# Linear attention and gated MLP on one core: query blocks in seven products for eight, and instruction orders computed from one program text

## The chip, the cores and the metric

One core of a Trainium2 chip. The metric is the device time of one execution in microseconds, lower is better. The kernel before takes 208.9 us (median of three runs, 208.53 to 208.99).

A core has TensorE (PE, matmuls into PSUM), VectorE (DVE), ScalarE (ACT), GpSimd (POOL) and SyncE (SP, which here only issues DMAs). Each runs its own list of instructions in order; between engines there are semaphores. PSUM is used as eight banks of 512 float32 columns per partition.

## What is computed

One input `x` of 2048 tokens by 640 features, bf16. A layer norm without weights gives `xn`, which goes two ways: linear attention with 32 heads of 20 features, and an MLP of width 1728 whose output, through silu, gates the attention's.

```python
xn = _layernorm(x)
q, k, v = split(xn @ wqkv)                       # 32 heads of 20
phi = lambda t: where(t > 0, t + 1, exp(t)) + 1e-6
pq, pk = phi(q), phi(k)
kv, z = einsum("bhsd,bhse->bhde", pk, v), einsum("bhsd->bhd", pk)
o = einsum("bhqd,bhde->bhqe", pq, kv) / (einsum("bhqd,bhd->bhq", pq, z)[..., None] + 1e-6)
s = o @ wo
g = silu(relu(xn @ w1) @ w2)
out = x + s * g
```

## The kernel before

Tokens are cut into 16 tiles `t` of 128, or four chunks `j` of 512. The work, in the order of TensorE:

- **Head.** `x` and weights are loaded; `bn`, `aggr` (statistics) and `LN_norm` (normalisation, VectorE) make `xn`; `xnT_dma` (L545) turns each tile by a transposing DMA on SP. Key tiles (`K_mm`, L551, ten matmuls of 320 columns) are evacuated by ScalarE twice, exp and relu (`K_evac`), and `K_fin` on VectorE adds them to `pk`. Hidden blocks (`H_mm`, L655) are five matmuls of 512 columns and a relu.
- **Hidden and query blocks.** Ten pairs of hidden feature tiles are computed in *units* (`h_unit`, L1002), each a two by two block product in seven products for eight (Winograd's form). Sums of weight blocks (`h_S`) and of `xnT` blocks (`h_T`) are made beforehand by VectorE in float16. A unit has seven steps: s1, s5, s6, s2, s7, s3, s4. It holds four PSUM banks; s1, s5 and s7 are followed by a copy on ScalarE, s6 and s4 by an addition on VectorE that reads PSUM. Query blocks (`Q_mm`, L607; feature tile `f` of five, chunk `j` of four: 20 blocks of five matmuls) and key tiles 8 to 15 stand between the steps as fillers, so that TensorE has work while the other engines evacuate. `Q_mm` is followed by exp and relu on ScalarE and two operations on VectorE.
- **Denominator and gram matrix.** `z_sum`, `z_col`, `den`, `den_rec`: the reciprocal of the denominator goes to DRAM and is read back spread over partitions (`den_store`, `load_recip`, chunk by chunk), and `divide` multiplies the queries by it. `xn`'s gram product with `pk` takes two units (`seven`, gram) and a last feature tile directly (L1580); from it and `wv`, `kv_group` and `W_block` build the attention's output weight `wf`, whose rows are put in place by ten small DMAs.
- **Output.** Eight pairs of token tiles: `U_steps` (MLP's second matmul, in seven products, gates by silu) and `O_steps` (attention output, in seven products, for pairs 1 to 6; tiles 0, 1, 14 and 15 directly by `s_tile` and `s_last`), then `s_mult` and `s_store` on VectorE and the output's DMA.

All orders are written out by hand: the Python code calls `sc.op`, `sc.group` and `sc.dma` in one sequence, and each engine gets its instructions in that sequence. `Sched` works out the waits at each call. `K_mm` with `whole=True` adds one matmul of 192 columns (L562) that only fills the rest of a bank.

The order around the first query block, after key tile 7 in the head: x load of tiles 10 and 11, hidden blocks 4, 5, 10, 11, 12 of chunk 1 with normalisation 8, x loads 12 to 15 and two w1 loads between them, `H_half`, then query blocks (0,0) and (0,1).

Of the kernel before, what the change touches and what calls it, by code (L numbers as in the profile page):

```python
# [11 lines left out]
class _Res:  # L12
    __slots__ = ("w", "r", "nread")

    def __init__(self):
        self.w = None
        self.r = {}
        self.nread = 0


class Sched:

    def __init__(self, nc, n_dma_sems):
        self.nc = nc
        self.ops = {E: [] for E in ENGS}
        self.count = {E: 0 for E in CENGS}
        self.gseq = 0
        self.seq_at = {E: [] for E in CENGS}
        self.seq_at_dma = []
        self.vc = {E: {} for E in ENGS}  # L30
        self.vc_at = {E: [] for E in CENGS}
        self.vc_at_dma = []
        self.res = {}
        self.ndma = 0
        self.dma_sem_of = []
        self.dsem_count = [0] * n_dma_sems
        self.dsem_last_k = [None] * n_dma_sems
        self.n_dma_sems = n_dma_sems
        self.allow_unread = set()

# [18 lines left out]
    def _require(self, E, agents, waits):  # L59
        need_eng = {}  # L60
        need_dma = []
        for a in agents:
            if self._known(E, a):
                continue
            if a[0] == "D":
                if a not in need_dma:
                    need_dma.append(a)
            else:
                if need_eng.get(a[0], -1) < a[1]:
                    need_eng[a[0]] = a[1]  # L70
        items = [("E", Ep, idx, self.seq_at[Ep][idx]) for Ep, idx in need_eng.items()] + \
                [("D", a[1], None, self.seq_at_dma[a[1]]) for a in need_dma]
        items.sort(key=lambda x: -x[3])
        for kind, a1, a2, _sq in items:
            if kind == "E":
                Ep, idx = a1, a2
                if self._known(E, (Ep, idx)):
                    continue
                waits.append(("E", Ep, idx + 1))
                vc = self.vc[E]  # L80
                vc[Ep] = max(vc.get(Ep, 0), idx + 1)
                self._merge(E, self.vc_at[Ep][idx])
            else:
                k = a1
                if self._known(E, ("D", k)):
                    continue
                si, val = self.dma_sem_of[k]
                waits.append(("D", si, val))
                self.vc[E][("D", k)] = True
                self._merge(E, self.vc_at_dma[k])  # L90

    def _hazards(self, R, W):
        agents = []
        for key in R:
            st = self.res.get(key)
            if st is not None and st.w is not None:
                agents.append(st.w)
        for key in W:
            st = self.res.get(key)
            if st is not None:  # L100
                if st.w is not None:
                    agents.append(st.w)
                agents.extend(st.r.values())
        return agents

    def _update_res(self, agent, R, W):
        Rset = set(R)
        for key in R:
            st = self.res.get(key)
            if st is None:  # L110
                st = self.res[key] = _Res()
            rk = agent if agent[0] == "D" else agent[0]
            st.r[rk] = agent
            st.nread += 1
        for key in W:
            st = self.res.get(key)
            if st is None:
                st = self.res[key] = _Res()
            else:
                assert (st.w is None or st.nread > 0 or key in Rset or key in self.allow_unread  # L120
                        or (agent[0] == "PE" and st.w[0] == "PE")), (
                    "unread overwrite of %r by %r (prev writer %r)" % (key, agent, st.w))
            st.w = agent
            st.r = {}
            st.nread = 0

    def op(self, E, fn, R=(), W=(), extra=()):
        return self.group(E, [fn], R, W, extra)

    def group(self, E, fns, R=(), W=(), extra=()):  # L130
        assert E in CENGS
        waits = []
        agents = self._hazards(R, W) + list(extra)
        self._require(E, agents, waits)
        idx = self.count[E]
        self.count[E] += 1
        self.vc_at[E].append(dict(self.vc[E]))
        self.seq_at[E].append(self.gseq)
        self.gseq += 1
        self.ops[E].append(("op", waits, fns, idx))  # L140
        self._update_res((E, idx), R, W)
        return (E, idx)

    def dma(self, E, fn, sem_idx, R=(), W=(), extra=()):
        waits = []
        agents = self._hazards(R, W) + list(extra)
        prev = self.dsem_last_k[sem_idx]
        if prev is not None:
            agents.append(("D", prev))
# [14 lines left out]
    def wait_all_dma(self, E, sem_idxs):  # L164
        waits = []
        for si in sem_idxs:
            k = self.dsem_last_k[si]
            if k is None:
                continue
# [1527 lines left out]
```

## Time and profile before

| what | value |
|---|---|
| median of 3 runs | 208.9 us |
| span of the profiled execution, first to last instruction | 207.0 us |
| last matmul ends | 204.5 us |
| matmuls | 1400 |
| granted TensorE clock, mean | 1.000 |

The span is what the page and the trace describe; the runs' times hold some 1.9 us around it. In a row of instructions the first two numbers are start and duration in us, counted from the span's start; where several are merged, the duration runs from the first's start to the last's end. Matmuls overlap in the pipe (one of 512 columns lasts 379 ns by its row), so the distance between starts, not the duration, is what one costs.

### The profile page before, as it was taken

The page shows a single profiled execution, that of the slowest core. Times are in us where ns is not written, and L with a number is a line of the kernel's source. Part 1 is how long each engine was busy: PE and PEld are TensorE (multiplying, and loading weights), DVE is VectorE, ACT ScalarE, POOL GpSimd, SP SyncE. Part 2 cuts the span into 40 slices and gives each one's busy share as a digit, 9 for nine tenths or more (in the row PEclk, how much of TensorE's full clock was granted, in tenths as well). Part 3 has the DMA queues.
Part 4 walks back from the last instruction along what each step waited for, and adds up shares of the span by engine and source line. Part 5 has one row for each costly group of instructions (what it writes and reads, how often), then busy time and mean ns, then how long its engine had stood idle before and what let it go on. Part 6 is the DMA issues. An engine that isn't in the chain of part 4 may idle for free.

```text
span 207.0 us, 3745 instructions
## 1 busy us (share of the span) xinstructions
PE 203.6 (98%) x1400; PEld 126.3 (61%) x1400; DVE 169.7 (82%) x373; ACT 124.3 (60%) x251; POOL 18.0 (9%) x53
## 2 busy tenths in 40 slices
PE   8999999999999999999999999999999999999995
PEld 7755645545555444444456777777777777777773
DVE  4888997988969787686889669898888989897465
ACT  5598869888889987686563435462525354352531
POOL 3174032101330000000000000000000000000001
PEclk9999999999999999999999999999999999999999
DMA  6965999211037000302225999237931011010103
GB/s 194 331 190 117 255 203 275 42 32 29 6 63 198 25 3 0 127 0 57 74 63 114 251 357 384 90 108 234 371 129 63 3 63 46 21 63 0 63 5 127
DMA packets 32999, 24.74 MB, mean 119 GB/s; under 512 B 12757, under 2 KB 32981, under 8 KB 32981
## 3 DMA queue, kind: packets, MB, share of 16 engines
q1 hardware_dynamic: 31749, 23.13, 39.2%
q10 hardware_dynamic: 1232, 1.37, 1.9%
q8 instruction: 11, 0.18, 0.4%
q14 instruction: 7, 0.06, 0.1%
HBM read 15.81 MB, written 5.24 MB: 102 GB/s over the span
## 4 chain that ended last, share of the span: by engine, by line
PE 97%; DMA 1%; DVE 1%; issue 0%
PE psT L882 40%; PE psT L1036 19%; PE psT L556 11%; PE psT L609 11%; PE psT L658 6%; PE psT L1529 3%; PE psT L1580 2%; DMA reg<-in_A_x_dram 1%; PE psT L676 1%; PE psT L1320 1%; PE psT L530 1%; PE psT L1294 1%; PE psT L756 1%; PE psT L786 1%; PE psT L432 0%; DVE stats L469 0%
## 5 line engine op out<-in xcount | busy, mean ns | idle before, releaser
L882 PE MATMUL psT<-reg,regH 128*128 128x320 bf16 (+1 forms) x224 | 34.3, 299 | 0.0
L882 PE MATMUL psT<-reg 128*128 128x320 bf16 (+1 forms) x164 | 27.7, 299 | 0.0
L882 PEld LDWEIGHTS psT<-reg,regH 128*128 128x128 bf16 (+1 forms) x224 | 21.9, 98 | 8.6
L1354 ACT ACTIVATE wv_sb<-psT 128x320 bf16<-128x320 f32 x28 | 11.3, 436 | 25.2 <-PE psT L882 15.4
L609 PE MATMUL psT<-reg 128*128 128x512 bf16 x100 | 24.4, 379 | 0.0
L1036 PE MATMUL psT<-reg 128*128 128x512 bf16 x80 | 23.2, 379 | 0.0
L827 DVE TENSOR_TENSOR psT<-psT,reg 128x320 f32<-128x320 f32 x30 | 14.3, 493 | 9.3 <-PE psT L882 9.2
L889 ACT ACTIVATE psT<-psT 128x320 f32<-128x320 f32 x32 | 13.6, 426 | 11.2 <-PE psT L882 10.7
L882 PEld LDWEIGHTS psT<-reg 128*128 128x128 f16 (+1 forms) x164 | 16.0, 98 | 6.9 <-DVE regH L827 0.2
L889 ACT ACTIVATE reg<-psT 128x320 f32<-128x320 f32 (+1 forms) x24 | 10.4, 435 | 15.6 <-PE psT L882 13.6
L556 PE MATMUL psT<-reg 128*128 128x320 bf16 x120 | 17.9, 299 | 0.0
L1042 ACT ACTIVATE psT<-psT 128x512 f32<-128x512 f32 x20 | 11.9, 595 | 8.2 <-PE psT L1036 8.2
L569 ACT ACTIVATE regE<-psT 128x640 bf16<-128x640 f32 x24 | 15.6, 706 | 1.9 <-PE psT L556 1.2
L609 PEld LDWEIGHTS psT<-reg 128*128 128x128 bf16 x100 | 9.6, 98 | 11.6 <-issue 0.7
L1048 ACT ACTIVATE regH<-psT 128x512 bf16<-128x512 f32 (+1 forms) x24 | 14.5, 604 | 2.1 <-PE psT L1036 1.8
L556 PEld LDWEIGHTS psT<-reg 128*128 128x128 bf16 x120 | 11.5, 98 | 6.5 <-ACT regE L569 0.5
L469 DVE BATCH_NORM_STATS2 stats<-reg 128x6 f32<-128x320 bf16 x32 | 14.1, 475 | 1.3 <-DMA reg<-in_A_x_dram 1.3
L827 DVE TENSOR_TENSOR reg<-reg 128x1024 f16<-128x1024 bf16 (+6 forms) x17 | 13.5, 805 | 1.7 <-DMA reg<-in_B_w_dram 1.2
L882 PE MATMUL psT<-reg,pqT 128*128 128x320 bf16 (+1 forms) x72 | 14.7, 299 | 0.0
L1517 DVE TENSOR_TENSOR reg<-psT,wv_sb 128x640 bf16<-128x640 f32 (+2 forms) x16 | 11.8, 739 | 3.0 <-PE psT L882 1.8
L1036 PEld LDWEIGHTS psT<-reg 128*128 128x128 bf16 x80 | 7.7, 98 | 9.4 <-issue 0.4
L1522 POOL TENSOR_TENSOR reg<-reg 128x224 bf16<-128x224 bf16 x1 | 0.6, 607 | 144.0 <-DVE reg L1517 144.0
(143 smaller groups left out, 369.0 us busy)
## 6 DMA issues: line engine op xcount, KB each, us to landing
reg<-in_B_w_dram SPq DMA_DIRECT2D x12, 320.0 KB, 5.5
scr<-rden SPq DMA_DIRECT2D x4, 640.0 KB, 8.3
reg<-in_A_x_dram SPq DMA_DIRECT2D x4, 640.0 KB, 6.6
out_dram<-reg SPq DMA_DIRECT2D x15, 160.0 KB, 1.9
regE<-scr SPq DMA_DIRECT2D x3, 640.0 KB, 7.5
reg<-in_A_x_dram SPq DMA_DIRECT2D x4, 320.0 KB, 4.4
reg<-in_A_wo_dram SPq DMA_DIRECT2D x6, 160.0 KB, 3.3
reg<-in_A_x_dram SPq DMA_DIRECT2D x5, 160.0 KB, 5.5
```

The lines of the kernel that those rows point to most:

```text
L469: sc.op("DVE", lambda eng: eng.bn_stats(stats[:, t, a, :], xv[:, HN * a:HN * (a + 1)]), R=[("xin", xs(t))], W=[("stats", t, a)])
L556: fns.append(lambda eng, a=a, k=k, lhs=lhs: eng.matmul(ps[b + a][:, 0:HN], lhsT=lhs, rhs=wk[:, k, HN * a:HN * (a + 1)], start=(k == 0), st ...
L569: sc.op("ACT", lambda eng: eng.activation(out=o_.rearrange("p (a n) -> p a n", a=2), in_=ps2(b, HN), func=func, scale=scale), R=[("ps", b) ...
L609: sc.group("PE", [(lambda eng, k=k: eng.matmul(ps[b], lhsT=wq[:, k, P * f:P * (f + 1)], rhs=xnT[:, j, k, :], start=(k == 0), stop=(k == C ...
L658: sc.group("PE", [(lambda eng, k=k: eng.matmul(ps[b], lhsT=w1_col(k, P * f, P), rhs=src[:, k, :], start=(k == 0), stop=(k == C - 1))) for ...
L827: sc.op("DVE", lambda eng: eng.tensor_tensor(out=out, in0=in0, in1=in1, op=op), R=R, W=W, extra=extra)
L882: sc.group("PE", [(lambda eng, k=k, lhs=lhs, rhs=rhs: eng.matmul(ps[b][:, 0:HN], lhsT=lhs, rhs=rhs, start=(start and k == 0), stop=(k == n ...
L889: sc.op("ACT", lambda eng: eng.activation(out=dst, in_=ps[b][:, 0:HN], func=ACTF.Copy), R=[("ps", b)], W=[dkey], extra=extra)
L1036: sc.group("PE", [(lambda eng, k=k, lhs=lhs, rhs=rhs: eng.matmul(ps[b], lhsT=lhs, rhs=rhs, start=(start and k == 0), stop=(k == n - 1), sk ...
L1042: sc.op("ACT", lambda eng: eng.activation(out=dst, in_=ps[b], func=ACTF.Copy), R=[("ps", b)], W=[dkey], extra=extra)
L1048: sc.op("ACT", lambda eng: eng.activation(out=dst, in_=ps[b], func=ACTF.Relu), R=[("ps", b)], W=[("hT", j, f)])
L1517: sc.op("DVE", lambda eng: eng.tensor_tensor(out=tmpo[:, os_, lo:hi].rearrange(shp, a=na), in0=src, in1=g_of(t)[0][:, lo:hi].rearrange(shp ...
```

## The change

It has one new algorithmic part and moves nearly all of the order.

- **Query units.** `q_unit(f, jp)`, for f of 0 and 1 and both chunk pairs, computes the blocks (f, f+2) by (2jp, 2jp+1) in seven products: sixteen of 20 query blocks. `q_S` makes the sums of `wq` blocks; the sums of `xnT` are those of the hidden units, of which there are now two sets (`hTv[0]`, `hTv[1]`). The four blocks of feature tile 4 stay direct. (`k_unit` and `m_unit`, for keys and a mixed pair, are defined and not used in the text.)
- **One program text.** After the head, `PROGRAM` lists the steps by name. `play` reads it word by word. Banks are no longer fixed: `take` gives the free bank that was used longest ago, units get the half of PSUM that is free.
- **Computed order.** Calls only record. `Sched.place` then goes through all records with a duration for each kind (`cost`) and takes, for ScalarE, VectorE and GpSimd, the next one among the first 60 recorded by earliest start and latest allowed time. TensorE and SP keep the order of the text, and so does everything of the head. Orders are static in the built kernel.
- **Key tiles 8 to 15 in halves** (`K_half`, 320 columns, one bank each; four ScalarE instructions a tile for two), without the `whole` matmul.
- **DMAs.** On SP, `n8` (normalisation 8 and its transposing DMA) comes ahead of x loads 10 to 15, `n9` ahead of x load 12, and so on, by the text. `wo` is loaded after w2 instead of early. `wv` comes in two parts. Reciprocals: do0, do1, rc0, do2, rc1, do3, rc2, rc3, with W_block's copies and the reload of `x` between them.
- **End.** Tile 14 (`st14`) comes after the last step of the last unit.

```diff
+    def place(self):
...
+            for E in ENGS:
...
+                if E in ("PE", "SP") or w[0].n < self.head:
+                    c = w[0]
...
+                else:
+                    can = [(max(free[E], ready[o.n]), o.late, o.n) for o in w[:self.LOOK] if not nleft[o.n]]
...
+                    est, late, n = min(can)
+                    c = recs[n]
+                    for e2, l2, n2 in can:
+                        if l2 < c.late and (e2 <= est or (e2 < est + c.occ and l2 < est + c.occ)):
+                            c, est2 = recs[n2], e2
...
+    LOOK = 60
...
+    if name in ("tensor_copy", "tensor_scalar", "memset"):
+        return (0.065 + 0.00105 * n, 0.15 + 0.00105 * n) if wide else (0.08 + 0.00026 * n, 0.16 + 0.00026 * n)
...
+            o.occ = 1.3 if o.turn else 0.5
...
+            o.dur = 2.7 if o.turn else 1.95 + o.byt
...
+PROGRAM = """
+H15 n8 xa H111 T0 xc n9 xb rb n10 H14 SQ H112 Q04 a1.s5 a1.s1 H110 p0.s5 wa Ka8 n11 wb a1.s6 n12 a1.s2 n13
+p0.s1 n14 a1.s7 a1.s3 p0.s2 SH1 a1.s4 Kb8 p0.s6 n15 Ka9 Kb9 p0.s3 a0.s1 Ka10 Q14 p0.s7 a0.s5 a0.s6 Kb10 a0.s2
+p0.s4 a0.s7 T1 hh0 Kb12 a3.s1 a0.s3 a0.s4 a3.s5 a3.s6 Ka11 a3.s2 Kb11 a3.s7 a3.s3 b3.s1 b3.s5 a3.s4 b3.s6
...
+H212 b1.s5 b1.s2 GS0 b1.s6 a2.s5 a2.s1 b1.s7 b1.s3 a2.s6 b1.s4 SH2 a2.s2 b0.s5 b0.s1 a2.s3 a2.s7 b0.s6 b0.s2
...
+b2.s3 b4.s1 b4.s5 b2.s4 g0.s5 w2b g0.s1 b4.s2 b4.s6 mv6 g0.s6 b4.s3 b4.s7 hh1 g0.s2 b4.s4 g0.s7 dn w2d g0.s3
+w2c g0.s4 c0 GS1 sl wo uSa0 g1.s1 g1.s5 g1.s6 g1.s2 g1.s7 g1.s3 g1.s4 wv1 wv0 do0 do1 c1 uT1 u0.s1 kv1 uT3 rc0
+uSb0 dv0 do2 rc1 kv0 uT2 uT4 u0.s5 u0.s6 W2 W5 u0.s2 W1 do3 u0.s3 oS1 W3 u0.s7 uSa1 W0 W4 xre u1.s1 uSb1 rc2
+dv1 uSa2 oT u0.s4 u1.s5 u1.s6 u1.s2 u2.s1 u1.s3 u1.s7 u2.s5 u1.s4 st1 st0 o1.s5 uSa3 u2.s2 o1.s1 oS2 u2.s6 rc3
...
+o5.s3 uSb7 u6.s4 o5.s4 u7.s1 o6.s5 u7.s5 o6.s1 u7.s6 o6.s2 u7.s2 o6.s6 u7.s7 o6.s3 o6.s7 u7.s3 o6.s4 u7.s4
+st14
+"""
...
+    def q_S(i):
+        A11, A12, A21, A22 = wq[:, 0:2, 0:2 * P], wq[:, 2:4, 0:2 * P], wq[:, 0:2, 2 * P:4 * P], wq[:, 2:4, 2 * P:4 * P]
...
+            tt(qSv[1], A21, A22, ALU.add, [("wq",)], [k(1)])
...
-    def h_unit(i, jp=1):
+    def unit(jp, blk, wkeys_, ws, skeys, out, out22, tile=None):
...
             1: (z([blk(0, 0), blk(0, 1)], xb(j0, 0)), w),
             2: (z([blk(0, 2), blk(0, 3)], xb(j0, 2)) + last(0, j0), w),
+            3: (z(ws(4), xb(j1, 2)) + last(0, j1), w + sk(4)),
+            4: (z([blk(1, 2), blk(1, 3)], tv(4)) + last(1, j0), w + [("hTs", jp, 4)]),
+            5: (z(ws(1), tv(1)), sk(1) + [("hTs", jp, 1)]),
+            6: (z(ws(2), tv(2)), sk(2) + [("hTs", jp, 2)]),
+            7: (z(ws(3), tv(3)), sk(3) + [("hTs", jp, 3)]),
             8: (last(1, j1), w),
...
+    def q_unit(f, jp):
+        o = P * f
+
+        def out(half, j, b):
+            both, sum_ = Q_evac(j, f + 2 * half, b)
+            both()
+            pend.append(sum_)
+
+        def out22(j, b, s5, skey):
+            tt(ps[b], ps[b], s5, ALU.add, [("ps", b), skey], [("ps", b)])
+            out(1, j, b)
...
+    def take(narrow=False):
+        can = [b for b in range(8) if held[b] is None and (b % 2 or not narrow)]
+        assert can, "no free bank"
+        b = min(can, key=lambda b: (last_use[b], b))
+        last_use[b] = step_no[0]
+        return b
...
+    def K_half(t, a):
+        b = take(True)
+        K_mm(t, [b, b], halves=(a, ))
+        for func, slot, key in ((ACTF.Exp, 0, "ek_e"), (ACTF.Relu, 1, "ek_r")):
+            sc.op("ACT", lambda eng, func=func, slot=slot: eng.activation(
+                out=ek[:, eks(t), slot, HN * a:HN * (a + 1)], in_=ps[b][:, 0:HN], func=func),
+                R=[("ps", b)], W=[(key, eks(t), 1)] if a else [(key, eks(t))])
...
+    def norm(t):
+        if t > 8:
+            S(t)
+        N(t)
...
+        "xa": lambda: x_load(10, 2),
+        "xb": lambda: x_load(12, 2),
+        "xc": lambda: x_load(14, 2),
...
+        "wv0": lambda: w_load(wv_sb[:, 0:2, :], A_wqkv[0:2 * P, 2 * D:3 * D], ("wv", 0), extra=hz([("s5h", 0)]), E="ACT"),
```

In the text `a` and `b` are hidden units on chunks 0 and 1, and 2 and 3; `p` and `q` query units likewise; `g` gram units; `u` and `o` output units; `Hjf` and `Qjf` direct blocks; `Ka8`, `Kb8` the halves of key tile 8; `rb` the row scales' four small matmuls (L943); `hh` the half feature tile; `T` and `SH`, `SQ` sums of `xnT` and of weights; `wa`, `wb` loads of w1; `dv`, `do`, `rc` divide, store and load of reciprocals.

## The prediction

> **What bounds the kernel now.** I read the page's busy table, its slices and its chain first, since they tell which engine sets the end.
>
> ```profile
> PE 203.6 (98%) x1400; PEld 126.3 (61%) x1400; DVE 169.7 (82%) x373; ACT 124.3 (60%) x251; POOL 18.0 (9%) x53
> ...
> PEclk9999999999999999999999999999999999999999
> ...
> PE 97%; DMA 1%; DVE 1%; issue 0%
> ```
>
> TensorE is busy for the whole span at the full granted clock and is 97% of the chain. A busy matmul row can still hide waiting, so next came the timeline of TensorE, for the distance from start to start.
>
> ```profile
> 40.80 0.57 PE L556 MATMUL psT<-reg 128*128 128x320 bf16 x3
> 41.21 0.25 PE L562 MATMUL psT<-reg,const-bfloat16-1.0 128*128 128x192 bf16 x1
> 41.29 0.60 PE L1036 MATMUL psT<-regX,pqT 128*128 128x512 f16 x2
> 41.73 0.81 PE L1036 MATMUL psT<-reg 128*128 128x512 bf16 x3
> 42.37 1.24 PE L609 MATMUL psT<-reg 128*128 128x512 bf16 x5
> 43.45 0.59 PE L1036 MATMUL psT<-regX,reg 128*128 128x512 f16 x2
> ```
>
> Five 512-column matmuls of L609 take 43.45 - 42.37 = 1.08 us, so 0.2165 us each; ten of 320 columns go by at 0.136 us each in the same way. Nothing stands between the groups. From about 8 us to 204.5 I find no hole over 0.2 us. TensorE's work is the time, then: what is taken from it is gained whole, what is not cannot be gained, and every new wait of TensorE is lost whole.
>
> **What is removed.** A query unit computes four of the 20 blocks (feature tiles f and f+2, token chunks j0 and j1) with 18 matmuls of 512 columns (products of 2, 3, 3, 3, 2, 2, 2 and 1) where direct blocks take 4 x 5 = 20. Four units save 8 x 0.2165 = 1.73 us. The `whole` matmul of L562 goes; the next start is 41.29 - 41.21 = 0.08 us later, four times: 0.32 us. I count the other matmuls of the program text against the loops: key halves, hidden units, gram units, `u` and `o` units, the four direct output tiles are as many as before. Floor: -2.05 us.
>
> **The first query block.** TensorE follows the text word by word. After the last key tile of the head it has H15, H111, the four matmuls of `rb`, H14, H112, then Q04. The rows that price this:
>
> ```profile
> 23.45 2.32 PE L658 MATMUL psT<-reg 128*128 128x512 bf16 x10
> 25.61 0.39 PE L943 MATMUL psT<-ident,rsyH 128*128 128x128 bf16 x4
> 25.83 3.40 PE L658 MATMUL psT<-reg 128*128 128x512 bf16 x15
> ...
> 26.15 1.28 SPq L546 DMA_TRANSPOSE reg<-reg  x1
> ...
> DMA to landing us min/median/max: 2.7/2.7/2.7
> ```
>
> Q04 is reached at 23.45 + 4 x 1.083 + 0.22 = 28.0 (in the old order a fifth H block, 1.19 us of `H_half` and so 30.36). It reads `xnT` of tiles 0 to 3. The last of these four transposing DMAs is issued at 26.15 and lands 2.7 later, at 28.87, and everything ahead of it on SP (two loads, three transposes) belongs to the head, which stays in its order. So TensorE waits 0.9 us. Bounds: 0, if the four land a microsecond earlier, as they may with fewer loads in flight, and 1.2 (their slowest neighbour was issued over 2.04 instead of 1.28). I take 0.9. The transposes that are moved ahead of loads (`n8` before `xa`, `n9` before `xb`) come behind these four on SP and can't help them; they help Ka8, 4.5 us after Q04, whose tile is due in time: `n8` issues at 27.5 instead of 28.10 and before the loads that stretched its landing.
>
> *A rule beside it.* The Trainium skill (Advanced Engine Details and Errata, X-Bar Transpose (TRN2)) says that transposing DMAs are as fast as plain ones. By that rule the wait is not there and the sum ends 0.9 lower. The trace speaks against it: 1.28 us on SP for a transpose of 160 KB, 0.43 to 0.58 for plain loads.
>
> **VectorE and ScalarE after the head.** The units add, each, three copies (0.60 us, 0.49 from start to start), two 512-column PSUM additions (0.70, 0.61 apart); the sums of `q_S` are four of 0.42. ScalarE: 12 x 0.49 = 5.9, and eight key tiles in halves, 8 x (4 x 0.33 - 2 x 0.59) = 1.1, both from the distances of such instructions in the timeline. VectorE: 8 x 0.61 + 4 x 0.35 = 6.3. Stages before:
>
> ```profile
> 26.00:54.60 28.60, 28.60 (x165) 14.26 (x164) 24.97 (x64) 23.54 (x44) 5.55 (x12) 1.00 0.48 106
> 54.60:111.00 56.40, 56.40 (x352) 27.93 (x351) 45.19 (x97) 43.22 (x81) 2.50 (x10) 1.00 0.20 56
> 111.00:124.00 13.00, 13.00 (x96) 9.17 (x95) 9.69 (x16) 4.13 (x10) 0.00 (x0) 1.00 0.99 281
> ```
>
> The columns are TensorE, weight loads, VectorE, ScalarE, GpSimd, clock, DMA share. The tight place is the first row: the text puts `b3.s5`, which needs tiles 8 to 15 transposed and the first sum of `T1`, 25.7 us of TensorE's work after Q04, at 54.6, where the old kernel began such units at 72. VectorE must do by then: K_fin of tiles 6 to 9, 4 x 0.77 = 3.1; eight norms 2.9; seven statistics 7 x 1.04 = 7.3; `T0` 2.5 and 0.6 of `T1`; nine weight sums 3.2; a1, a0 and a3's first sum 3.6; p0 with four block sums 3.9; one of the two single blocks' and p0's six sums may hang over by three: 1.3 - 2.0. Together 26.4 of 28.6 us (92%, 87% before). It fits, if what can wait does wait: all that is recorded ahead of `b3.s5` is 32.7. On SP `wa` and `wb` now stand behind `n10` and `n11`, so behind those normalisations, near 40; landed by 45, their sums (1.4) are done by 47, and a3.s5, the first to read them, comes at 50. Bounds of VectorE's term: 0 and 32.7 - 28.6 - 0.9 = 3.2. I take 0, since at 87% the row shows no wait of TensorE.
>
> **The middle.** DMA share 0.99 in the third row: this stage now also gets `wo` (6 x 160 KB, 2.95 us of issue on SP, before at 62) and keeps w2, `wv`, the stores. The reciprocal stores go do0, do1, rc0, do2, rc1, do3, each load behind its store on SP; W_block's ten copies (0.74 each) queue behind rc1 and do3. Who waits: `dv0` and `oT` for st1 and o1, about 145; before, the chunk-0 reciprocal landed at 122.7 and the last W copy at 142 at most: over 3 us of cover. The value weights, `wv`, are nearest to the edge: issued at 118.3, 9.0 to land, used at 128.9. Now they go as two parts; the one of 320 KB waits for the gram unit that keeps its s5 copy there, until 112 if that is g0 or 123.2 if it is g1. With the 4.4 that a 320 KB load took it is in by 127.6 at the latest, and kv1 comes at 128.07 - 2.05 + 0.9 + 0.95 (`u0.s1`) = 127.9. Bounds 0 and 3 (the 9.0 row); I take 0. The silu table (1.28 us on ScalarE) moves to where ScalarE is busy 4.13 of 13.
>
> **The end.** Before:
>
> ```profile
> 202.23 0.82 DVE L1517 TENSOR_TENSOR reg<-psT,wv_sb 128x640 bf16<-128x640 f32 x1
> 203.09 0.49 DVE L1522 TENSOR_TENSOR reg<-reg 128x640 bf16<-128x640 bf16 x1
> 203.70 1.21 DVE L1517 TENSOR_TENSOR reg<-psT,wv_sb 128x224 bf16<-128x224 f32 x3
> 204.94 0.37 DVE L1522 TENSOR_TENSOR reg<-reg 128x416 bf16<-128x416 bf16 x1
> ```
>
> Tile 14 came before the last unit's `s4`, so VectorE could multiply it at 202.23, ahead of the last 15 matmuls (202.96). In the text st14 is the last word: its product is free only 0.2 after 202.96 in the old times, then 0.82, its addition 0.49, three pieces in 0.95 without gaps, 0.37: 205.8 instead of 205.31. Cost 0.45; bounds 0.2 and 0.8 (VectorE still busy with tile 13).
>
> **The sum.** -1.73 - 0.32 + 0.9 + 0.45 = -0.70, from 207.05 to 206.35 in this profiled execution. Its span lies 1.85 under the median of the runs, 208.9, and what lies around it doesn't change: **208.2**.
>
> **Rivals.**
> (1) *No wait at Q04*: the four transposes land early. For it: with no other DMA around they land 2.6 after issue and nothing but two loads delays the first; against it: those loads are unchanged. 208.2 - 0.9 = 207.3. The skill's rule above ends here; its own part of the chance is small, the rows being against it.
> (2) *Short waits between the products*. Between s6 and s7 of a unit VectorE must read and add (0.70, and some 0.2 from TensorE's end to its start). Before, s2 and a Q block lay between, 43.45 - 41.73 = 1.72. In the text it is 1.08 at most places and 0.87 at b1. A VectorE operation under way (0.45 on average) delays it; ten places by 0.07 give 0.7: 208.9, no change.
> (3) *VectorE takes over in the stage to `b3.s5`*. The order is computed with fixed durations, with N at 0.25 where the trace has 0.36, and is then static; once one transpose or one normalisation is late, TensorE stands. It decides when more than 29.5 us are in front of that step. 29.5 is 28.6 and the 0.9 that the wait at Q04 gives. With half of what could wait done ahead the demand is (26.4 + 32.7) / 2 = 29.6 and 8 x 0.1 = 0.8 for N: 0.9 too much; with three quarters 2.4 too much; the middle is 1.6: 208.2 + 1.6 = 209.8, slower. Against it: 26.4 is below 28.6.
>
> **Chances.** Forecast (208.2, itself 207.7 to 208.5) 0.42, (1) 0.23, (2) 0.17, (3) 0.18. What can be told from no change is 0.2%, 0.42 us, so from 208.48 to 209.32. Faster: 0.42 + 0.23 less 0.01 at the edge = 0.64; same 0.18; slower 0.18. The range from 207.0 (under it only if the end costs nothing too) to 209.8 leaves out one tenth on each side.
>
> **What would show it.** Matmuls of the query line 20 and four more units of 18; L562 gone; a hole of 0.9 us ahead of the first query block at 28, ended by the transposing DMA; no holes to 55; VectorE's last chain 0.45 longer after TensorE's last matmul. Wrong: TensorE's holes above 1.5 us in all (then VectorE's row of waits says which), or kv1 waiting for `wv`.

## The result, and the profile after

214.57 us, median of 4 runs (214.44 to 214.86), against 208.72 us (208.19 to 208.99) for the kernel before on the same chip: 1.0268 times as long, 95% interval 1.0219 to 1.0317. The forecast was 208.2 with a range of 207.0 to 209.8, so both its direction and its range were wrong. The profiled execution spans 213.08 us instead of 207.05.

The page of the kernel after, busy table, granted clock and chain:

```profile
PE 204.0 (96%) x1377; PEld 122.5 (58%) x1388; DVE 170.5 (80%) x385; ACT 130.7 (61%) x279; POOL 17.9 (8%) x53
...
PEclk9999999999999999999999999999999999999999
...
PE 38%; DVE 30%; DMA 12%; ACT 7%; issue 5%; POOL 5%; SPq 2%; DVEq 0%; ACTq 0%
```

The clock is as before. The weight loads went from 1400 to 1388 (the matmul rows miss a few records, so the weight loads are counted): eight matmuls of the query units and four of L562 are gone, as worked out. But the chain, 97% TensorE before, now goes through VectorE, DMAs, ScalarE and GpSimd: TensorE waits for all of them in turn.

Where? Two stages, first the kernel before, then after. Columns: TensorE, weight loads, VectorE, ScalarE, GpSimd (busy us, instructions), clock, DMA share, GB/s.

```profile
26.00:56.00 30.00, 30.00 (x171) 14.88 (x170) 26.30 (x67) 24.94 (x46) 6.41 (x14) 1.00 0.46 101
145.00:175.00 30.00, 30.00 (x223) 21.56 (x222) 26.89 (x60) 12.52 (x33) 0.00 (x0) 1.00 0.31 108
```

```profile
26.00:56.00 30.00, 27.81 (x155) 12.93 (x155) 28.25 (x77) 25.23 (x56) 7.75 (x21) 1.00 0.52 117
145.00:175.00 30.00, 28.51 (x203) 18.87 (x202) 25.86 (x59) 11.06 (x28) 0.00 (x0) 1.00 0.52 175
```

TensorE, full in both stages before, gets 15 weight loads less done in the first and 20 less in the second. The busy figure hides the first 0.15 us or so of each hole, so from here on I take holes from the starts of the weight loads: the time from one matmul group to the next, less the group's own matmuls at 0.216 us for 512 columns and 0.136 for 320. By stage, after 8 us, for this kernel and those of the experiments below (the stage from 60 to 111 us holds about 1 us in each that is no waiting but changes between matmul shapes; where a group lies across a stage's border, an entry shifts by up to 0.3 us, while the sum of a row hardly does). Counted in the same way, the kernel before has 0.2, 0.6, 0.1 and 0.0 us in these stages.

| kernel | 26-60 | 60-111 | 111-145 | 145-175 | last matmul to end | span |
|---|---|---|---|---|---|---|
| after | 3.33 | 2.27 | 0.43 | 2.63 | 3.24 | 213.1 |
| GpSimd durations | 1.71 | 2.07 | 0.41 | 2.66 | 3.24 | 211.3 |
| all durations | 0.90 | 1.99 | 0.29 | 2.52 | 3.25 | 210.4 |
| queue | 3.46 | 2.27 | 0.25 | 1.16 | 3.24 | 211.7 |
| H110 ahead of Q04 | 3.12 | 2.27 | 0.17 | 2.58 | 3.23 | 212.4 |
| tail | 3.09 | 2.11 | 0.28 | 2.56 | 2.55 | 212.6 |
| all repairs | 0.97 | 2.22 | 0.0 | 0.18 | 2.55 | 206.8 |
| all repairs but H110 | 0.73 | 2.38 | 0.0 | 0.18 | 2.56 | 207.1 |

**The two largest holes of the first stage**, in the timeline of TensorE of the kernel after (start, us, instruction; in brackets the idle time ahead and what ended it):

```profile
26.27 1.67 PE L788 MATMUL psT<-reg 128*128 128x512 bf16 x7
28.77 1.25 PE L754 MATMUL psT<-reg 128*128 128x512 bf16 x5 [0.83 <-DMA reg<-reg]
...
33.34 1.24 PE L1183 MATMUL psT<-reg 128*128 128x512 bf16 x4
35.52 0.61 PE L1183 MATMUL psT<-regX,reg 128*128 128x512 f16 x2 [0.94 <-DVE psT L954]
```

The first is Q04, foreseen: 0.99 us from start to start against 0.9. The second, 1.10 us, is step s7 of the hidden unit a1, which takes over the bank of s6 after VectorE's addition in PSUM. What VectorE did meanwhile:

```profile
33.29 0.45 DVE L643 TENSOR_SCALAR reg<-reg,mv,rsy 128x640 bf16<-128x640 bf16 x1 [0.46 <-POOL rsy L632]
33.65 0.88 DVE L624 BATCH_NORM_STATS2 stats<-reg 128x6 f32<-128x320 bf16 x2
34.45 0.41 DVE L954 TENSOR_TENSOR regH<-reg,regH 128x512 f16<-128x512 bf16 x1
34.77 0.69 DVE L954 TENSOR_TENSOR psT<-psT,wv_sb 128x512 f32<-128x512 f32 x1
```

The addition (34.77) stands behind a normalisation, two statistics and a weight sum, though by the plan's own latest allowed times they are due 1.4 to 5.3 us after it. VectorE was even idle for 0.46 us ahead of the normalisation, waiting for GpSimd's power. `place` has these five in the same order, with other times: normalisation 31.53, statistics 31.78 and 32.17, weight sum 32.56, addition 32.90. On the chip the normalisation began 1.76 us later than that and the addition 1.87, while TensorE, up to this point, was only 0.83 behind the plan (s6 at 32.91 for 32.09). The plan gives every GpSimd operation 0.25 us from start to start; the group of the power (busy us, mean ns of one, idle before) says

```profile
L632 POOL TENSOR_TENSOR rsy<-rsv,mhalf 128x1 f32<-128x1 f32 x16 | 9.6, 609 | 1.1
```

0.609 on average. An instruction that comes late by an error of the plan holds up all that stand behind it, since the order is static.

**The largest hole of the second stage** is ahead of the direct tile st0 at 151.36 (0.95 idle, ended by ScalarE's `gate_q`; 1.11 from start to start). The gate waited for an addition of VectorE, here at 150.01:

```profile
147.66 0.89 DVE L954 TENSOR_TENSOR reg<-reg 128x640 f16<-128x640 bf16 x2 [1.63 <-DMA reg<-reg]
148.47 0.62 DVE L954 TENSOR_TENSOR regH<-regH 128x896 f16<-128x896 bf16 x1
149.01 0.48 DVE L954 TENSOR_TENSOR reg<-reg 128x640 f16<-128x640 f16 x1
149.41 0.28 DVE L954 TENSOR_TENSOR reg<-pqT,reg 128x256 f16<-128x256 bf16 x1
149.61 0.48 DVE L954 TENSOR_TENSOR reg<-reg 128x640 f16<-128x640 bf16 x1
150.01 0.49 DVE L954 TENSOR_TENSOR psT<-psT,reg 128x320 f32<-128x320 f32 x1
```

The 640-column instructions are `o_T`. Its first two wait 1.63 us for the last copies of `W_block`; the addition stands behind all four. The plan has `o_T` at 141.10, 6.6 us earlier, when TensorE is some 4.3 behind the plan. What SP issued (second column: the time that the issues took):

```profile
136.10 3.66 SPq L1607 DMA_DIRECT2D reg<-reg  x5
139.81 0.62 SPq L933 DMA_DIRECT2D scr<-rden  x1
140.47 5.27 SPq L1607 DMA_DIRECT2D reg<-reg  x5
145.78 2.53 SPq L1822 DMA_DIRECT2D reg<-in_A_x_dram  x4
148.35 0.51 SPq L942 DMA_DIRECT2D regE<-scr  x1
```

Ten copies and do3 (L933) take 9.6 us, 0.54 to 2.1 us a copy, where the plan has 0.5. Behind them come the reload of `x`, then rc2 (L942), which landed at 158.68, 10.3 us after its issue. The kernel before issues rc1 and rc2 (L815 there) ahead of all copies (L1335), and had rc2 in at 131.80:

```profile
122.66 3.53 SPq L815 DMA_DIRECT2D regE<-scr  x2
132.50 7.62 SPq L1335 DMA_DIRECT2D reg<-reg  x10
```

In the kernel after, VectorE waits 1.50 us for rc2, until 158.70, and three more holes of TensorE follow, 0.24 at 160, 0.43 at 162 and 0.39 at 170; all three are gone where rc2 goes out earlier (experiment 3). A wait of the same kind is most of the 0.43 us between 111 and 145: at 133.01 VectorE had waited 0.96 us for rc0 with a division, and three operations that bring `kv`'s products out of PSUM stand behind it; the first matmuls of `W_block` wait for them, 0.34 us, until 134.89.

**The tail** grew from 2.55 to 3.24 us. VectorE after TensorE's last matmuls (these end at 209.84):

```profile
207.35 0.49 DVE L1786 TENSOR_TENSOR reg<-reg 128x640 bf16<-128x640 bf16 x1
208.51 1.40 DVE L1781 TENSOR_TENSOR reg<-psT,wv_sb 128x640 bf16<-128x640 f32 x3 [0.66 <-PE psT L1793]
209.83 0.83 DVE L1786 TENSOR_TENSOR reg<-reg 128x640 bf16<-128x640 bf16 x1
210.59 0.36 DVE L1781 TENSOR_TENSOR reg<-psT,wv_sb 128x208 bf16<-128x208 f32 x1
210.98 0.38 DVE L1786 TENSOR_TENSOR reg<-reg 128x416 bf16<-128x416 bf16 x1
```

Tile 14's product starts when its last matmul is through, as worked out, and its addition then stands between the pieces of tile 15; here, beside a GpSimd addition (209.71 to 210.31), it lasted 0.83 us instead of 0.49.

### The profile page after: what moved, and what is told of

It is laid out like the page before. It is cut to its first block, busy times and chain, and to the rows that moved or that the text cites. A ratio compares the mean times of both kernels' runs of the same rounds, so it can differ in the third digit from the quotient of the medians.

```text
span 213.1 us, 3736 instructions
## 1 busy us (share of the span) xinstructions
PE 204.0 (96%) x1377; PEld 122.5 (58%) x1388; DVE 170.5 (80%) x385; ACT 130.7 (61%) x279; POOL 17.9 (8%) x53
## 4 chain that ended last, share of the span: by engine, by line
PE 38%; DVE 30%; DMA 12%; ACT 7%; issue 5%; POOL 5%; SPq 2%; DVEq 0%; ACTq 0%
PE psT L1010 19%; PE psT L1183 12%; DMA regE<-scr 5%; DVE reg L954 4%; DVE stats L624 4%; POOL rsy L632 3%; DVE psT L954 3%; DMA reg<-scr 3%; DMA scr<-rden 3%; DVE pqT L947 2%; PE psT L703 2%; PE psT L587 2%; DVE regE L954 2%; ACT pqT L767 2%; POOL rsv L630 2%
## 5 line engine op out<-in xcount | busy, mean ns | idle before, releaser
L1183 PE MATMUL psT<-reg 128*128 128x512 bf16 (+1 forms) x138 | 38.1, 380 | 0.5
L1010 PE MATMUL psT<-reg,regH 128*128 128x320 bf16 (+1 forms) x224 | 35.4, 299 | 0.3 <-DVE reg L1781 0.3
L954 DVE TENSOR_TENSOR psT<-psT,reg 128x320 f32<-128x320 f32 (+1 forms) x33 | 16.8, 517 | 9.5 <-PE psT L1010 8.1
L1183 PEld LDWEIGHTS psT<-reg 128*128 128x128 bf16 (+1 forms) x144 | 13.4, 98 | 17.6 <-DVE psT L954 1.2
L954 DVE TENSOR_TENSOR reg<-reg 128x1024 f16<-128x1024 bf16 (+6 forms) x24 | 17.1, 718 | 2.5 <-DMA reg<-reg 1.6
L1190 ACT ACTIVATE psT<-psT 128x512 f32<-128x512 f32 x28 | 17.1, 647 | 0.9 <-PE psT L1183 0.9
L703 PEld LDWEIGHTS psT<-reg 128*128 128x128 bf16 x120 | 11.3, 98 | 7.4 <-ACT regE L713 0.5
L1781 DVE TENSOR_TENSOR reg<-psT,wv_sb 128x640 bf16<-128x640 f32 (+2 forms) x16 | 11.6, 736 | 4.0 <-PE psT L1010 3.3
L765 ACT ACTIVATE regE<-psT 128x512 bf16<-128x512 f32 x20 | 12.7, 651 | 3.1 <-PE psT L754 1.5
L767 ACT ACTIVATE pqT<-psT 128x512 bf16<-128x512 f32 x20 | 13.2, 661 | 0.0
L954 DVE TENSOR_TENSOR psT<-psT,wv_sb 128x512 f32<-128x512 f32 (+1 forms) x15 | 10.2, 679 | 3.6 <-ACT regE L1454 1.7
```

Of the source, the lines that this page charges most:

```text
L703: fns.append(lambda eng, a=a, k=k, lhs=lhs: eng.matmul(ps[bk[a]][:, 0:HN], lhsT=lhs, rhs=wk[:, k, HN * a:HN * (a + 1)], start=(k == 0), st ...
L765: exps.append(sc.op("ACT", lambda eng: eng.activation(out=e_, in_=ps[b], func=ACTF.Exp), R=[("ps", b)], W=[("er_e", es)]))
L767: sc.op("ACT", lambda eng: eng.activation(out=pqT[:, f, schunk(j)], in_=ps[b], func=ACTF.Relu), R=[("ps", b)], W=[("pqT", j, f)], extra=hz ...
L954: sc.op("DVE", lambda eng: eng.tensor_tensor(out=out, in0=in0, in1=in1, op=op), R=R, W=W, extra=extra)
L1010: sc.group("PE", [(lambda eng, k=k, lhs=lhs, rhs=rhs: eng.matmul(ps[b][:, 0:HN], lhsT=lhs, rhs=rhs, start=(start and k == 0), stop=(k == n ...
L1183: sc.group("PE", [(lambda eng, k=k, lhs=lhs, rhs=rhs: eng.matmul(ps[b][:, 0:nn], lhsT=lhs if tile is None else rhs, rhs=rhs if tile is Non ...
```

## The experiments

Two theories. *Order*: the computed order rests on durations and landing times that the chip doesn't have; a few VectorE instructions placed too early and a few DMAs queued too late stop TensorE, and what is in the text doesn't matter much. *Load*: the text gives VectorE and ScalarE so much before 56 us that no order of theirs helps.

**1. Durations.** Only the numbers that `place` works with; the instructions are the same.

```diff
     if E == "POOL":
-        return 0.25, 0.3
+        return (0.57, 0.62) if k.get("op") == ALU.pow else (0.22, 0.24)
...
+    if name == "tensor_scalar" and n == 640 and hasattr(k.get("scalar2"), "shape"):
+        return 0.36, 0.44
...
-            o.occ = 1.3 if o.turn else 0.5
+            inside = a[0].tensor.name == a[1].tensor.name
+            o.occ = 1.3 if o.turn else 0.8 if inside else 0.5
-            o.byt = 0.6 if o.turn else size / (205e3 if a[0].tensor.name == "scr" else 350e3)
+            o.byt = 0.6 if o.turn else size / (205e3 if a[0].tensor.name == "scr" else 225e3 if a[1].tensor.name == "scr" else 350e3)
...
-                line = max(est + (2.0 if c.turn else 1.5), line + (0.6 if turned and not c.turn else 0.0)) + c.byt
+                line = max(est + (2.0 if c.turn else 1.9), line + (0.6 if turned and not c.turn else 0.0)) + c.byt
```

> Only the durations that the order is computed from change, to what the traces show: GpSimd's power 0.57 instead of 0.25, a normalisation 0.36 instead of 0.25, loads 0.4 later, reads of the reciprocal at 225 instead of 350 KB/us, copies inside SBUF 0.8 on SP instead of 0.5. Text, work and DMAs stay. Order theory (the computed order is static and rests on durations that are too short, so what is late stands in front of what is urgent): more than half of the 7.2 us that TensorE waits in the changed kernel go, 209 to 211. Load theory (VectorE and ScalarE have too much to do in the stage, whatever the order): less than 1 us is gained, 213.5 to 214.6.

212.66 us (211.96 to 213.02), 1.0206 (1.0178 to 1.0234); span 210.4, 2.6 less than after. (The profiled execution was the fastest of four; by the medians, each against the kernel before on its chip, it is 1.7 less.) VectorE around the place of the 1.10 us hole now:

```profile
32.51 0.49 DVE L627 BATCH_NORM_STATS2 stats<-reg 128x6 f32<-128x320 bf16 x1
33.05 0.45 DVE L646 TENSOR_SCALAR reg<-reg,mv,rsy 128x640 bf16<-128x640 bf16 x1
33.41 0.69 DVE L957 TENSOR_TENSOR psT<-psT,wv_sb 128x512 f32<-128x512 f32 x1
34.01 0.48 DVE L627 BATCH_NORM_STATS2 stats<-reg 128x6 f32<-128x320 bf16 x1
```

The addition comes right behind the normalisation, the other statistics and the weight sum follow it, and the hole is gone. The stage from 26 to 60 us falls from 3.33 to 0.90. The stage from 145 us on does not move (2.52): this is why the time fell between what the two theories said.

**2. GpSimd's durations alone** (the first two lines of that diff).

> Of the durations only GpSimd's power (0.57 for 0.25) and its small addition (0.22 for 0.25) are changed. Order theory, with GpSimd the duration that is most wrong: the waits between 28 and 60 us go, 2 to 4 us: 210.5 to 212.5. If the DMA durations matter more: 213.5 to 214.5. Load theory: 214 to 214.6.

213.13 us (213.06 to 213.46), 1.0236 (1.0216 to 1.0256); span 211.3. The time lies between the ranges expected: part of the waits went, not all. 3.33 becomes 1.71 in the first stage. Of this, 0.45 is Q04's wait, 0.54 here for 0.99, which the durations don't set: the head's order is the same in all these kernels, and only its DMA landed earlier in this execution (28.26 for 28.72). Without Q04, 2.3 us become 1.2, and 0.45 with all durations: one wrong constant is some 60% of what the durations are worth there.

**3. Queue alone.**

```diff
-uSb0 dv0 do2 rc1 kv0 uT2 uT4 u0.s5 u0.s6 W2 W5 u0.s2 W1 do3 u0.s3 oS1 W3 u0.s7 uSa1 W0 W4 xre u1.s1 uSb1 rc2
+uSb0 dv0 do2 do3 rc1 rc2 kv0 uT2 uT4 u0.s5 u0.s6 W2 W5 u0.s2 W1 u0.s3 oS1 W3 u0.s7 uSa1 W0 W4 xre u1.s1 uSb1
```

> Only SP's queue: do3 goes out behind do2, rc2 behind rc1, both ahead of the ten W copies and of the reload of x, as in the kernel before. Queue theory (the waits of TensorE behind 145 us, 1.1 at the first direct output tile and 0.4 twice later, come from W copies and the third reciprocal that land late): 1 to 2.5 us less, 212 to 213.5. If these waits come from the order of VectorE alone: 214 to 214.8.

213.05 us (212.44 to 214.58), 1.024 (1.0192 to 1.0287); span 211.7, as expected of the queue. From 145 us on 2.63 becomes 1.16, and nothing before moves by more than 0.2. One hole of 1.06 is left at 151.6: VectorE now has the divisions by the early reciprocals (L947) ahead of the product that frees a direct tile's bank (L1781).

```profile
150.40 1.55 DVE L947 TENSOR_TENSOR pqT<-pqT,regE 128x1536 bf16<-128x1536 bf16 x2
151.87 1.55 DVE L1781 TENSOR_TENSOR reg<-psT,wv_sb 128x640 bf16<-128x640 f32 x2
```

**4. H110 ahead of Q04.**

```diff
-H15 n8 xa H111 T0 xc n9 xb rb n10 H14 SQ H112 Q04 a1.s5 a1.s1 H110 p0.s5 wa Ka8 n11 wb a1.s6 n12 a1.s2 n13
+H15 n8 xa H111 T0 xc n9 xb rb n10 H14 SQ H112 H110 Q04 a1.s5 a1.s1 p0.s5 wa Ka8 n11 wb a1.s6 n12 a1.s2 n13
```

> Only the text: H110 ahead of the first query block instead of two steps behind it. The hole of 1.0 us at 28 goes. If lateness there throws the static orders behind it out, more goes with it (the 1.1 at 34): 212.5 to 213. If each wait has its own cause: 213.5. If the lateness of the transposes only shows up one step later: 214.5.

214.87 us (214.16 to 215.73), 1.033 (1.0293 to 1.0368): by the median nothing is gained. TensorE's timeline in the profiled execution, the fastest of four:

```profile
28.74 1.24 PE L754 MATMUL psT<-reg 128*128 128x512 bf16 x5
...
33.30 0.61 PE L1183 MATMUL psT<-reg 128*128 128x512 bf16 x2 [0.26 <-ACT regE L1454]
34.83 0.39 PE L1183 MATMUL psT<-regX,reg 128*128 128x512 f16 x1 [0.92 <-DVE psT L954]
```

No wait at Q04 any more; 0.43 of it is back 4 us later, where ScalarE has to read the key half first, and s7 of a1 waits for the same addition, until 34.83 instead of 35.52. In all the stage has 3.12 instead of 3.33. A wait of TensorE early on is also slack for VectorE's late order: what is taken from one is paid at the next.

**5. Direct query blocks** instead of the units.

```diff
-        return unit(jp, lambda half, k: wq[:, k, o + 2 * P * half:o + 2 * P * half + P], [("wq",)],
...
+        def block(j, f_, b):
+            def step():
+                both, sum_ = Q_mm(j, f_, b)
+                both()
+                pend.append(sum_)
+            return step
+
+        return dict(s1=block(2 * jp, f, base + 1), s5=block(2 * jp, f + 2, base + 3), s6=none,
+                    s2=block(2 * jp + 1, f, base + 2), s7=block(2 * jp + 1, f + 2, base), s3=none, s4=none, base=base)
```

> Undo the first part of the change alone: each of the four query units becomes four direct query blocks at the places of four of its seven steps, with the unit's own banks; the three query sums on VectorE, the unit's scaled copies and its PSUM additions go, and twelve matmul groups come back (some 2 us of TensorE). The computed order and the queues stay. Load theory (the units' extra work on VectorE and ScalarE is what makes TensorE wait): the waits before 105 us go, which is more than the 2 us that come back: 211 to 213.5. Order theory (the waits come from an order computed with wrong durations, whatever is in it): the matmuls come back in full and the waits stay: 216 to 219.

220.87 us (220.2 to 223.4), 1.0579 (1.0494 to 1.0664): neither. The load theory's gain is far off, and it is worse than the order theory had it. New holes explain that; the first:

```profile
43.30 1.24 PE L754 MATMUL psT<-reg 128*128 128x512 bf16 x5
45.72 1.25 PE L754 MATMUL psT<-reg 128*128 128x512 bf16 x4 [1.18 <-ACT pqT L767]
```

Two blocks follow each other in places made for unit steps, and the second has to wait until ScalarE has read the first one's bank twice. This happens again at 96.9 us (1.34 each time from start to start). Two longer ones stand behind them, 1.66 us until 50.65, where an s7 waits for VectorE's addition, and 1.81 until 106.27, where a step waits for a copy of ScalarE. So the run says that the text is fitted to the units; it doesn't give the price of a unit against four blocks.

**6 and 7. All repairs**: 1, 3, 4 and, for the tail, tile 14's matmuls ahead of the last step of the last unit; and the same without 4.

```diff
-o5.s3 uSb7 u6.s4 o5.s4 u7.s1 o6.s5 u7.s5 o6.s1 u7.s6 o6.s2 u7.s2 o6.s6 u7.s7 o6.s3 o6.s7 u7.s3 o6.s4 u7.s4
-st14
+o5.s3 uSb7 u6.s4 o5.s4 u7.s1 o6.s5 u7.s5 o6.s1 u7.s6 o6.s2 u7.s2 o6.s6 u7.s7 o6.s3 o6.s7 u7.s3 o6.s4 st14
+u7.s4
```

> All the repairs at once: the plan's durations for the GpSimd power, the normalisation and the DMAs as the trace has them; do3 and rc2 ahead of the W copies and the x reload; H110 ahead of Q04; the last output tile's matmuls ahead of the last unit step. Order theory: the gains found one by one (1.9 for the durations, 1.5 for the queue, some 0.4 for the tail) are of different waits and add up: 209.5 to 211. Load theory: TensorE is short of work that is ready wherever the order is mended, and the gains overlap: 211.5 to 213.

> As the run with all the repairs, but Q04 left ahead of H110. Order theory: Q04 waits 0.4 us for its DMA, as it did with the corrected durations alone, against a wait of 0.3 after the move: within 0.5 us of the run with all repairs, 209.5 to 211. If the early place of Q04 is worth its wait, this is the faster of the two.

209.07 us (208.28 to 210.2, 10 runs), 1.0016 (0.998 to 1.0052), and 208.94 us (208.59 to 210.23, 10 runs), 1.0007 (0.9973 to 1.004), beside 208.35 (207.82 to 210.43) for the kernel before. Both are below the 209.5 to 211 that the order theory had, since the gains more than add up. By stage, the holes before 60 us shrink as with the durations alone (0.73 and 0.97 for 0.90) and the tail as in experiment 8 below: different waits, whose gains add up. From 145 us on the holes fall to 0.18, where the durations alone left 2.52 and the queue alone 1.16; there both are needed. H110 does nothing here either: with it Q04's wait is gone, and one of 0.44 for the key half stands at 32.7; without it Q04 waits 0.35. The stages of the kernel with all repairs:

```profile
26.00:56.00 30.00, 29.40 (x165) 14.33 (x167) 29.45 (x80) 27.36 (x59) 7.49 (x20) 1.00 0.47 109
145.00:175.00 30.00, 30.00 (x222) 21.16 (x220) 27.45 (x60) 12.36 (x31) 0.00 (x0) 1.00 0.35 120
```

VectorE is busy 29.45 of 30 us, with all of the change's work in it, and TensorE loses 0.6 of busy time instead of 2.2: the load fits, just. And the 1.11 hole ahead of st0 is gone, the two tiles' twenty matmuls run as one:

```profile
145.71 2.88 PE L1796 MATMUL psT<-reg,pqT 128*128 128x320 bf16 x20
```

**8. Tail alone.**

> The changed kernel with only the output tile 14's matmuls put ahead of the last step of the last hidden unit, as a test of the tail alone. If the 0.7 us that the tail gained in length is the order of these last groups, 213.8 to 214.3; if the tail is set by the last store and its DMA, no change, 214.4 to 214.9.

213.72 us (212.89 to 214.23), 1.0202 (1.0131 to 1.0273); a little under what was expected. Last matmul to end: 2.55 us, as in the kernel before. The 0.7 us were the order of the last groups.

**9 and 10. Two other texts** on top of durations, queue and tail, in each some thirty steps a few places earlier or later. The first line of the first:

```diff
-H15 n8 xa H111 T0 xc n9 xb rb n10 H14 SQ H112 Q04 a1.s5 a1.s1 H110 p0.s5 wa Ka8 n11 wb a1.s6 n12 a1.s2 n13
+H15 n8 xa H111 T0 xc xb n9 rb n10 H14 SQ H112 H110 Q04 a1.s5 a1.s1 p0.s5 wa Ka8 n11 wb a1.s6 n12 a1.s2 n13
...
```

> The repaired kernel (durations, queue, tail) with some thirty steps of the text moved by a few places, so that a replay of the static order with 2% longer ScalarE and VectorE work and 0.4 us later DMAs loses less. The repaired kernels still wait some 1.8 us ahead of 105 us. Order theory: about half of that goes, 208.0 to 208.7, a little under the kernel before. Load theory: VectorE is busy for 98% of the stage from 26 to 56 us, no text helps, 208.8 to 209.6.

> The same with another such text, in which H110 and the ninth tile's transposing DMA stand behind the loads again. Order theory: 208.0 to 208.7. Load theory: 208.8 to 209.6. The better of the two texts is the one whose Q04 waits less, if the early stage decides.

209.63 us (208.56 to 210.86, 12 runs), 1.0057 (1.0032 to 1.0082), and 209.23 us (208.5 to 210.71, 12 runs), 1.0033 (1.0011 to 1.0054). Both missed what the order theory had: 1.19 and 1.57 us of holes from 26 to 60 us instead of 0.73 to 0.97. In the first a wait of 0.44 for the key half stands where 4 had put one; in the second Q04 waits 0.76 for its DMA, and yet this text is not the slower of the two, against what was expected. For what is left in that stage the times are about the load theory's: these moves did not mend it. Two texts don't show that none can.

**11. Less to do for VectorE**, with the order made by the plan of the change.

```diff
-        sc.op("DVE", lambda eng: eng.bn_aggr(mv[:, t, :], stats[:, t, :, :].rearrange("p a b -> p (a b)")),
-              R=[("stats", t, 0), ("stats", t, 1)], W=[("mv", t)])
+        na = 1 if t > 8 else 2
+        sc.op("DVE", lambda eng: eng.bn_aggr(mv[:, t, :], stats[:, t, 0:na, :].rearrange("p a b -> p (a b)")),
+              R=[("stats", t, a) for a in range(na)], W=[("mv", t)])
...
-        bn(t, 1)
+        if t <= 8:
+            bn(t, 1)
```

> The changed kernel, durations and queue as they were, with less for VectorE to do early on: the statistics of tiles 9 to 15 are taken from half of each row (seven of 32 statistics instructions left out, 7 x 0.40 = 2.8 us of VectorE ahead of 50 us). Load theory (VectorE is full there, whatever the order): the waits between 30 and 60 us, 2.7 us in all, go nearly whole, 211.7 to 212.5. Order theory (an addition that TensorE waits for stands behind others because the plan had them start earlier): the waits get shorter by chance at most, 213.3 to 214.6.

214.53 us (213.33 to 215.24), 1.0278 (1.0235 to 1.032): nothing gained. The kernel leaves out the second half of each row in these statistics, so that VectorE had 2.8 us less to do, and still, ahead of the same step s7:

```profile
32.67 0.45 DVE L645 TENSOR_SCALAR reg<-reg,mv,rsy 128x640 bf16<-128x640 bf16 x1 [0.46 <-POOL rsy L633]
33.04 0.42 DVE L956 TENSOR_TENSOR regH<-regH,reg 128x512 f16<-128x512 f16 x1
33.37 0.42 DVE L956 TENSOR_TENSOR reg<-reg 128x512 f16<-128x512 bf16 x1
33.71 0.48 DVE L624 BATCH_NORM_STATS2 stats<-reg 128x6 f32<-128x320 bf16 x1
...
34.70 0.69 DVE L956 TENSOR_TENSOR psT<-psT,wv_sb 128x512 f32<-128x512 f32 x1
```

VectorE idles for GpSimd's power, then does what stands ahead of the addition; TensorE waits 0.91 us there and 2.72 in the stage, where of the 0.6 less than after Q04's DMA accounts for 0.4. This run and the repairs decide it together: with less load and the wrong order the waits stay, with the full load and a right order most of them go.

## Why the prediction was wrong, point by point

**What was right.** TensorE's removed work, -2.05: the weight loads are twelve fewer, and where TensorE doesn't wait its groups follow each other at the old distances. Q04: 0.99 us against 0.9, for the reason given: the last of the four transposing DMAs was issued at 26.02 and landed at 28.72. That the size fits so well is in part luck: with the same head and Q04 in its place, the other kernels wait between 0.35 and 1.12 us there, as that DMA lands between 28.13 and 29.18; and the upper bound of 1.2 does not follow from the row it names, which gives 0.87 + 2.04 - 1.28 = 1.6. Rival (1), no wait there, fell. The rule set beside it, that of the Trainium skill (Advanced Engine Details and Errata, X-Bar Transpose (TRN2)) that such DMAs go as fast as plain ones, was taken to mean no wait; the trace has 0.99. That does not refute the rule: from issue to landing this DMA took 2.70 us, loads of `x` 2.4 to 5.9. What takes longer is the issue on SP, 1.28 us against a median of 0.58 (0.40 to 1.36). But experiment 4 shows that Q04's 0.9 could not be booked by itself, since its removal gained 0.2 of it in the trace, and nothing by the median.

**The tail**, 0.45 with bounds 0.2 and 0.8: right mechanism, 0.69 measured (3.24 - 2.55), and gone when the order of the groups is turned. The size was off because the moved addition met GpSimd's and lasted 0.34 longer; the sum had it at 0.49.

**The step that failed first: VectorE's term, taken as 0 of 0 to 3.2.** The sum of work, 26.4 of 28.6 us (92%), was what must be done; the repaired kernel's VectorE is busy for 29.45 of 30 (98%), work that could wait included. But whether it fits was not the question. I asked what VectorE must do, and not in which order `place` would put it. That the order is static and computed with short durations I had as rival (3), with the right stage, the right mechanism and a chance of 0.18; I priced it as an overflow of work (1.6 us) and only N's 0.25 against 0.36 entered. GpSimd's 0.25 stood in the same function, with the power's 0.62 in the profile before, and I did not compare them; it alone makes 1.2 us (2.3 - 1.2, both without Q04's wait). Of the 3.33 us in this stage Q04 is 0.99; the rest, 2.3, is what the term was worth.

**The second: the middle, taken as 0 of 0 to 3.** 3.1 us (0.43 + 2.63). In the prediction each transfer is held against the time at which its reader is due, with over 3 us of cover for `dv0` and `oT`, and no further. The reader was not the only one who waited. A VectorE instruction that waits for a DMA holds the engine, and behind `oT` stood a PSUM addition that the gate and then st0 needed. Nor did I compare the plan's 0.5 us for a copy on SP with the 0.74 that I used myself: ten copies with do3 among them took 9.6 us, and `oT` was put 6.6 us too early. `kv1` and `wv`, which I had thought nearest to the edge, did not wait: st0, with no term of its own, did.

**Third, 60 to 111 us**: four holes, 1.0 us, where the sum had none. Two, 0.27 at 73.3 and 0.25 at 97.3, are rival (2) as described, an s7 that waits for the addition on s6 because VectorE was in the middle of something else; the rival's mechanism, at two places instead of ten. The others, 0.38 at 99.2 and 0.13 at 103.9, wait for ScalarE's copies of products: at 99.2 ScalarE had been working without a pause since 86.0, at 103.9 it had just loaded the silu table:

```profile
102.18 1.28 ACT L1842 ACT_TABLE_LOAD   x1
103.47 0.20 ACT L1842 ACTIVATE msum<-zero 128x1 f32<-128x1 bf16 x1
103.58 0.58 ACT L1190 ACTIVATE psT<-psT 128x512 f32<-128x512 f32 x1
```

I had put its new place down at nothing, because ScalarE is idle on average in the stage from 111 us on. The plan put it earlier, at 98.39, and here too a duration was wrong: `cost` gives this instruction of one column 0.05 us and does not know of the load. None of the repairs touched these four.

Together -2.05 + 0.99 + 0.69 + 2.3 + 3.1 + 1.0 = 6.0, as the spans differ by (213.08 - 207.05 = 6.03).

**What stays open.** With all repairs the kernel does 2.05 us less on TensorE and takes the same time as before: about 0.7 to 1.0 us of holes before 60 us and 1.0 after eat it. Whether a text exists that has neither is open. What a query unit is worth against four blocks under an order that suits both was not measured, and no run separates the key tiles in halves or the free choice of banks from the rest of the change.

## What to carry to other kernels

When an order is computed, compare every duration in the planner with the profile, the engines that are hardly busy first: GpSimd's power at 0.25 for 0.61, on an engine that is busy for 8%, was the costliest wrong duration here (1.2 us). Look also for work that the planner's list does not hold, like the table load. Then price each wait of an in-order engine by what stands behind it, and not by the instruction that waits. And a full TensorE row before a change says nothing of the slack that the others' order had; here two microseconds of its work were taken out, and with the order mended they came back as waits.

## What the runs showed of the hardware

**One copy within SBUF** of the ten held SP's queue for 2.1 us, in this kernel and in the one with the durations, in both the second copy behind do3; the others took 0.54 to 0.96, in the kernel before 0.55 to 0.99. Where do3 goes out ahead of all copies (queue, all repairs) the longest is 0.97 and 1.04. Why is not shown. **ScalarE's instructions look longer when they follow each other without a pause**: 512 columns from PSUM took 0.60 on average before and 0.65 to 0.67 after, up to 0.84 in one row, at an unchanged 0.475 us or so from start to start:

```profile
96.93 0.81 ACT L765 ACTIVATE regE<-psT 128x512 bf16<-128x512 f32 x1
97.41 0.82 ACT L767 ACTIVATE pqT<-psT 128x512 bf16<-128x512 f32 x1
97.88 0.84 ACT L1190 ACTIVATE wv_sb<-psT 128x512 f32<-128x512 f32 x1
```

So the mean of such rows is no measure of their cost. The busy time counts what overlaps only once: with rows cut to 0.60 (512 columns) and 0.44 (320), its rise from 124.3 to 130.7 us would be 6.0 instead of 6.4. **A VectorE addition beside a GpSimd addition**: the one of 640 bf16 columns in the tail, started at 209.83 while GpSimd added from 209.71 to 210.31, lasted 0.83 us instead of 0.49, as if it had begun to work at the other's end. The Trainium skill (SBUF — State Buffer, "SBUF: two separate sides") says that the two engines share a pair of ports as an exclusive lock, so that a VectorE instruction with two inputs in SBUF waits until a GpSimd instruction that reads SBUF and started first is through. This row agrees: it ended at 210.66, 0.35 after GpSimd's. The multiplications with one input in PSUM that ran beside GpSimd's addition in the kernel with all repairs (203.90 to 204.50) were not longer: three in 1.20 us, as in the kernel before (1.21). The addition lasts 0.83 us in all seven kernels in which tile 14 comes last and 0.49 in the six others, where it ends before GpSimd's begins; no run was made to test it by itself. GpSimd's instructions on one or two columns show nothing of the kind: 47 VectorE additions of this form that began within the last 0.28 us of one took 0.47 to 0.49.
